# A Fourier mixing layer and a snake MLP on one Trainium2 core: the second DFT stage forward, from batch 2 on, on mirrored sums and differences in quarters of the array

## The chip, the core and the metric

The kernel runs on one core of a Trainium2 chip. The metric is device time in microseconds of one execution, and what counts is the median of several. A core has five engines with one instruction queue each: TensorE (PE in the profile; PEld is its weight load), VectorE (DVE), ScalarE (ACT), GpSimd (POOL) and SyncE (SP). An instruction waits at the head of its engine's queue until the semaphores that it names are set, and what is queued behind it waits too. In this kernel SP and POOL issue nearly all DMA transfers.

## What is computed

```python
x: (8, 3008, 256); filt_r, filt_i: (1505, 256)
X = rfft(x, axis=1)                        # along the 3008 tokens of each batch
y = irfft(X * (filt_r + 1j*filt_i), n=3008, axis=1)
h = y.reshape(24064, 256) @ w_in           # 256 -> 2048
g = h + sin(alpha*h)**2 / (alpha + 1e-9)   # snake
out = g @ w_out                            # 2048 -> 256, float32
```

## The kernel before

3008 is 47 x 64, so each transform of a batch is two matrix products with a filter between the forward and the inverse pair:

- *First stage* (`first` for batch 1 at L203, `first_tiled` from batch 2 on at L214): a DFT over 47 rows. Its 48 result rows per token group (24 frequencies s, real and imaginary) go through PSUM into `t1_h`, and by DMA into the DRAM scratch `d1`.
- *Second stage forward* (`forward`, L238): a DFT over the 64 tokens n of a group, on rows loaded back from `d1` (`load_t2`, L233). For each of the 24 s there is one full 128x128 matmul of 256 columns against the table `d_t`: real and imaginary part of 64 tokens in, real and imaginary part of 64 frequencies out. Two s are evacuated together (L246, ACT) into `xf`, and two DMAs swap its halves into `xs` (L250).
- *Filter* (`product` L253, `cross` L261, all on DVE): p = xf * f0, then xs = xs * f1 and p = p + xs, on tiles of 128x512 in fp16, 12 of each per batch.
- *Inverse* (`inverse_tiled`, L284, from batch 2 on): the second stage back. 16 matmuls of 64x64 in the four quarters of the array, three such bursts per batch, evacuated by ACT (three) and DVE (one), then by DMA to the scratch `d2`. `load_t4` (L304) reads it back and `last` (L309) does the DFT over 47; its result lies in `y`.

The MLP is the main loop. 48 chunks of 512 (or, at every sixth place, 384) tokens take 8 steps each. A step does two blocks of `hidden` (L594): two matmuls `ph` of 512 columns, ACT takes the sine into `cos_all` (L605), and DVE forms `v` (L606) from that and from `ph` in PSUM. It also does one eighth of `project` (L610) of the chunk before: in most steps 8 matmuls `po` of 256 columns. A batch is 48 steps. While the MLP of one batch pair runs, the transforms of later batches are put between the steps.

What sets the order: nothing is scheduled at run time. `put(at, fn)` (L671) gives each piece of a transform a due step; `slot` (L735) records what is due twice per step, behind the two `hidden` blocks and behind the `project`, and takes at most one TensorE piece each time. The due steps are written out in `firsts` (L674), `inverses` (L679) and the loop at L701 to L732; `clear` (L685) moves `last` and `forward` away from the bursts in quarters of the array, and `aside` (L689) moves DVE pieces that would be due up to 1.1 steps ahead of a burst to just behind it. Each engine then takes its instructions in the recorded order.

PSUM: `hps` has 4 buffers, used in turn by the `ph` blocks and by the second half of each burst (2 buffers); `fps` has 2, for the first half of a burst, for `forward` and `last`; `ops` has 2, for `po`. So two `ph` blocks recorded behind a burst reuse the buffers of the two blocks recorded just ahead of it.

For batch 2, which has the least room, the due steps are: `first_tiled` 37.5 to 43.5, `load_t2` 45, `forward` from 51 on. For batch b from 4 on, with z = 48 b: `first_tiled` z-105.5 to z-81.5, `load_t2` from z-77 on every 12 steps, `forward` from z-65 on every 4 steps, `inverse_tiled` at z-46.5, z-30.5 and z-14.5.

Of the kernel before, what the change touches and what calls it, by code (L numbers as in the profile page):

```python
# [24 lines left out]
FUSED = 1  # L25
TILED = 2


def dft_tables():
# [22 lines left out]
    f16 = np.float16  # L52
    wf, wi = wf.reshape(N1 * 2, 2, NS, 2), 2 * wi.reshape(2, NS, 2, NR)
# [13 lines left out]
    return (eh.astype(f16), wh.reshape(NK, NR).astype(f16), wt.reshape(128, 64).astype(f16), wf.transpose(0, 2, 1, 3).reshape(NR, NK).astype(f16), wi.reshape(NK, NR).astype(f16), d,  # L67
# [4 lines left out]
def kernel(  # L72
# [11 lines left out]
    eh_host, wh_host, wt_host, wf_host, wi_host, d_host, wf0_host, wi0_host, e_host = dft_tables()  # L84
    eh_dram = nc.inline_tensor(eh_host, name="eh_tbl")
    wh_dram = nc.inline_tensor(wh_host, name="wh_tbl")
# [23 lines left out]
    t2pool = pool("t2", 4)  # L110
    xfpool = pool("xf", 3)
    ppool = pool("pp", 7)
    xspool = pool("xs", 3)
# [31 lines left out]
    eh_t = e_t[:, 0:NS // 2].rearrange("p a (b m) -> p (a b) m", m=64)  # L145
# [10 lines left out]
    def load_x(b, ch):  # L156
        xt = xpool.tile([128, 8, C], FP16, name=f"x_{b}_{ch}", tag="x")
        if b >= TILED:
            for h in range(2):
                ins = nc.gpsimd.dma_start(  # L160
                    out=xt[64 * h:64 * h + N1],
                    in_=bass.AP(tensor=x.tensor, offset=x.offset + (b * S + 32 * h + ch * 8) * C,
                                ap=[[64 * C, N1], [1, 8 * C]]))
                after(ins, marks["snake"])
            return xt
# [23 lines left out]
    class Spectral:  # L189

        def __init__(self, b):
# [6 lines left out]
            self.fused = b >= FUSED  # L198
# [15 lines left out]
        def first_tiled(self, ch):  # L214
            r0 = 8 * (ch % 2)
            for q in range(2):
                own, tag = (hps, "h") if q else (fps, "f")
                ps = [own.tile([128, 512], FP32, name=f"pa_{self.b}_{ch}_{q}_{h}", tag=tag) for h in range(2)]
                for h in range(2):
                    for c in range(2):  # L220
                        n = 4 * c + 2 * q
                        nc.tensor.matmul(out=ps[h][64 * c:64 * c + 64, :], lhsT=wt_t[64 * h:64 * h + N1],  # L222
                                         rhs=self.x[ch][64 * h:64 * h + N1, n:n + 2, :], start=True, stop=True)
                for h in range(2):
                    evac(t1_h[ch // 2][:, r0 + 4 * h + 2 * q:r0 + 4 * h + 2 * q + 2, :], ps[h], h == 0)
            d1 = self.d1.rearrange("a (h n) c -> a h (n c)", h=2)
            for c in range(2):
                n0 = (8 * ch + 4 * c) * C
                nc.sync.dma_start(out=d1[:, :, n0:n0 + 4 * C],
                                  in_=t1_h[ch // 2][64 * c:64 * c + 2 * NS, r0:r0 + 8, :]  # L230
                                  .rearrange("a (h n) c -> a h (n c)", h=2))

# [5 lines left out]
        def forward(self, u):  # L238
# [6 lines left out]
            self.xf[u] = xfpool.tile([128, 2, C], FP16, name=f"xf_{b}_{u}", tag="xf")  # L245
            nc.scalar.copy(out=self.xf[u], in_=ps)  # L246
            if self.fused:
                self.xs[u] = xspool.tile([128, 2, C], FP16, name=f"xs_{b}_{u}", tag="xs")
                for p in range(2):
                    nc.sync.dma_start(out=self.xs[u][64 * p:64 * p + 64, :, :],  # L250
                                      in_=self.xf[u][64 - 64 * p:128 - 64 * p, :, :])

        def product(self, u):  # L253
            self.p[u] = []
            for k in range(1 if self.fused else 2):
                pt = ppool.tile([128, 2, C], FP16, name=f"p_{self.b}_{u}_{k}", tag="p")
                marks["prod", u] = nc.vector.tensor_tensor(out=pt, in0=self.xf[u],  # L257
                                                           in1=f_t[k][:, 2 * u:2 * u + 2, :], op=ALU.mult)
                self.p[u].append(pt)

        def cross(self, u):  # L261
            xs, p = self.xs[u], self.p[u][0]
            nc.vector.tensor_tensor(out=xs, in0=xs, in1=f_t[1][:, 2 * u:2 * u + 2, :], op=ALU.mult)  # L263
            nc.vector.tensor_tensor(out=p, in0=p, in1=xs, op=ALU.add)  # L264

        def inverse(self, w):
            b = self.b
            pr = self.p.pop(w)
# [3 lines left out]
            for i in range(2):  # L272
                for k, pt in enumerate(pr):
                    nc.tensor.matmul(out=ps[:, i, :], lhsT=e_t[:, 2 * w + i, :],
                                     rhs=pt[:, i, :], start=(k == 0), stop=(k == len(pr) - 1))
            i0 = 2 * (w % 3)
            evac(self.g[:, i0:i0 + 2, :], ps, True if b == 1 else None)
# [5 lines left out]

        def inverse_tiled(self, w):  # L284
            g = gpool.tile([128, 4, 2, C], FP16, name=f"gt_{self.b}_{w}", tag="g")
            for q in range(2):
                own, tag = (hps, "h") if q else (fps, "f")
                ps = [own.tile([128, 2, C], FP32, name=f"pc_{self.b}_{w}_{q}_{k}", tag=tag) for k in range(2)]
                for i in range(2):
                    for k in range(2):  # L290
                        for c in range(2):
                            u = 4 * w + 2 * c + q
                            nc.tensor.matmul(out=ps[k][64 * c:64 * c + 64, i, :],  # L293
                                             lhsT=eh_t[64 * k:64 * k + 64, 2 * u + i, :],
                                             rhs=self.p[u][0][64 * k:64 * k + 64, i, :], start=True, stop=True)
                for k in range(2):
                    evac(g[:, 2 * q:2 * q + 2, k, :], ps[k], (q, k) != (1, 1))
            rows = self.d2.rearrange("a n c -> (a n) c").rearrange("(z p) c -> p z c", p=64)
            for c in range(2):
                z0 = 16 * w + 8 * c  # L300
                nc.sync.dma_start(out=rows[:, z0:z0 + 8, :],
                                  in_=g[64 * c:64 * c + 64].rearrange("p j k c -> p (j k) c"))
# [6 lines left out]
        def last(self, u):  # L309
# [8 lines left out]
            evac(y[:, cb, self.b % 2, n0:n0 + 4, :], psv)  # L318

# [167 lines left out]
    def forward_0(i):  # L487
# [5 lines left out]
        own, tag = (xspool, "xs") if i % 2 else (xfpool, "xf")  # L493
        xf0[i] = own.tile([128, 4, 128], FP16, name=f"xf_0_{i}", tag=tag)
# [141 lines left out]
    def load_half_table():  # L636

        after(nc.sync.dma_start(out=eh_t, in_=eh_dram.ap()), marks["snake"])

    put_later = [(54, load_half_table)]  # L640
# [33 lines left out]
    def firsts(b):  # L674

        return {2: (37.5, 39.5, 41.5, 43.5), 3: (49.5, 54.5, 60.5, 66.5)}.get(
            b, [48 * b - 105.5 + 8 * ch for ch in range(4)])

    def inverses(b):  # L679

        return (63.5, 73.5, 81.5) if b == 2 else [48 * b - 46.5 + 16 * w for w in range(3)]

    bursts = [at for b in range(TILED, B) for at in (*firsts(b), *inverses(b))]
# [108 lines left out]
```

## Time and profile before

| | |
|---|---|
| median of 3 runs | 779.78 us (777.6 to 784.53) |
| profiled execution: time, span in the profile | 779.97 us, 778.2 us |
| mean granted TensorE clock | 0.997 |
| TensorE, VectorE, ScalarE, GpSimd busy in the span | 98%, 85%, 78%, 48% |
| TensorE matmuls | 6039 |
| DMA bytes | 101.49 MB |
| step 0 to the last step | 38.4 us to 763.5 us |

The profile lists busy time by engine, by line and by operation, waits (who waited for what, how long, how often), the chain of work that ended last, and a timeline that merges equal instructions which follow each other (start, length from the first start to the last end, how many, and the idle time before them in brackets). Matmuls are pipelined: a row's length includes the way through the array, so the time that a group of them takes of TensorE is read from its start to the start of the next group.

### The profile page before, as it was taken

To read this page: it belongs to the slowest core of one execution; us is meant where nothing else is said; L and a number is where in the kernel's file an instruction comes from. 1 tells how busy PE (TensorE), PEld (TensorE's weight loads), DVE (VectorE), ACT (ScalarE), POOL (GpSimd) and SP (SyncE) were. 2 spreads that over 40 slices of the span, in tenths; PEclk is the share of its full clock that TensorE was granted. 3 is DMA by queue.
4 is the path that set the end of the run, shared out by engine and by line. 5 is a ranking of instruction groups with operands and counts; after the bars stand their busy time and mean duration, and the time that the engine had idled before them with its cause. 6 is when DMAs were issued, how large, how long until landed. Compare 5 with 4: busy or idle time off the path is not lost.

```text
span 778.2 us, 17224 instructions
## 1 busy us (share of the span) xinstructions
PE 763.9 (98%) x6039; PEld 517.3 (66%) x6039; DVE 658.2 (85%) x1173; ACT 610.5 (78%) x1203; POOL 371.2 (48%) x649
## 2 busy tenths in 40 slices
PE   8999999999999999999999999999999999999997
PEld 4757766666666666666666666766666666766665
DVE  6986998999988888898889988899888888787773
ACT  5798888898888877888878787788778787777762
POOL 6355554634555655455464647554464655430000
PEclk9999999999999999999999999999999999999999
DMA  9955578854765428644474536764254332411112
GB/s 227 264 110 158 119 179 240 223 137 124 188 164 133 124 58 215 157 108 128 108 202 111 141 93 147 198 150 121 72 145 111 85 72 56 135 46 34 36 41 56
DMA packets 81518, 101.49 MB, mean 130 GB/s; under 512 B 18884, under 2 KB 60864, under 8 KB 81431
## 3 DMA queue, kind: packets, MB, share of 16 engines
q0 software_dynamic: 27440, 47.29, 25.9%
q1 hardware_dynamic: 53434, 52.79, 25.3%
q8 instruction: 47, 0.77, 0.4%
q10 hardware_dynamic: 557, 0.31, 0.2%
q14 instruction: 40, 0.33, 0.1%
HBM read 56.15 MB, written 46.66 MB: 132 GB/s over the span
## 4 chain that ended last, share of the span: by engine, by line
PE 91%; DVE 4%; DMA 2%; ACT 1%; issue 1%; ACTq 0%; POOLq 0%; DVEq 0%
PE po L620 40%; PE ph L601 40%; DVE v L606 3%; PE pd L316 2%; PE pb L243 2%; PE pa L222 2%; PE pc L293 1%; PE pc L513 1%; DMA w<-in_moe_alpha_dram 1%; PE warm L437 1%; DMA d<-t_h 1%; ACT cos_all L605 1%; PE pb L491 1%; DMA t<-d 1%; PE pa L459 1%
## 5 line engine op out<-in xcount | busy, mean ns | idle before, releaser
L606 DVE SCALAR_TENSOR_TENSOR v<-cos_all,ph 128x512 f16<-128x512 f32 (+1 forms) x768 | 482.7, 671 | 96.9 <-ACT cos_all L605 93.1
L605 ACT ACTIVATE cos_all<-ph 128x512 f32<-128x512 f32 (+1 forms) x768 | 413.7, 599 | 100.3 <-PE ph L601 99.8
L665 POOL DMA_DIRECT2D out_dram<-o x530 | 292.5, 558 | 241.8 <-ACT o L630 212.6
L601 PE MATMUL ph<-y,w 128*128 128x512 f16 (+1 forms) x1536 | 389.1, 375 | 1.3 <-DVE v L606 1.1
L620 PE MATMUL po<-w,v 128*128 128x256 f16 x3008 | 389.3, 273 | 0.0
L620 PEld LDWEIGHTS <-v 128*128 128x128 f16 x3008 | 290.1, 98 | 84.2 <-issue 1.1
L601 PEld LDWEIGHTS <-w 128*128 128x128 f16 x1536 | 143.2, 98 | 113.9 <-issue 19.0
L630 ACT COPY o<-po 128x512 f32<-128x512 f32 x94 | 55.9, 595 | 7.6 <-PE po L620 7.3
L246 ACT CAST xf<-pb 128x512 f16<-128x512 f32 x84 | 50.9, 606 | 2.2 <-PE pb L243 1.4
L185 ACT CAST y<-pd 128x376 f16<-128x376 f32 (+1 forms) x86 | 41.9, 490 | 12.2 <-PE pd L316 8.8
L160 POOL DMA_DIRECT2D x<-in_x_dram x48 | 25.6, 539 | 40.5 <-DVE v L606 26.7
L185 ACT CAST t_h<-pa 128x512 f16<-128x512 f32 (+1 forms) x60 | 32.8, 589 | 12.5 <-PE pa L222 11.3
L316 PEld LDWEIGHTS <-t_a 96*128 96x128 f16 x448 | 31.4, 97 | 12.7
L264 DVE TENSOR_TENSOR p<-p,xs 128x512 f16<-128x512 f16 x84 | 35.7, 425 | 2.9
L263 DVE TENSOR_TENSOR xs<-xs,filt_t 128x512 f16<-128x512 f16 x84 | 35.1, 418 | 1.6 <-DMA xs<-xf 1.5
L257 DVE TENSOR_TENSOR p<-xf,filt_t 128x512 f16<-128x512 f16 x84 | 35.0, 418 | 0.0
L185 ACT CAST gt<-pc 128x512 f16<-128x512 f32 x54 | 28.1, 594 | 8.4 <-PE pc L293 8.4
L187 DVE CAST t_h<-pa 128x512 f16<-128x512 f32 (+1 forms) x52 | 33.5, 682 | 0.2
L243 PE MATMUL pb<-t,d_t 128*128 128x256 f16 x168 | 32.1, 273 | 0.8 <-DMA t<-d 0.8
L316 PE MATMUL pd<-wh_t,t_a 96*128 96x94 f16 x384 | 31.8, 204 | 0.0
L235 POOL DMA_DIRECT2D t<-d x28 | 24.4, 873 | 13.2 <-DMA d<-t_h 11.2
L243 PEld LDWEIGHTS <-d_t 128*128 128x128 f16 x168 | 16.3, 98 | 15.3 <-DMA t<-d 1.0
(70 smaller groups left out, 277.9 us busy)
## 6 DMA issues: line engine op xcount, KB each, us to landing
t<-d POOLq DMA_DIRECT2D x28, 384.0 KB, 5.2
xs<-xf SPq DMA_DIRECT2D x168, 64.0 KB
t_a<-d SPq DMA_DIRECT2D x28, 384.0 KB
x<-in_x_dram POOLq DMA_DIRECT2D x50, 188.0 KB, 4.4
d<-t_h SPq DMA_DIRECT2D x48, 192.0 KB
d<-gt SPq DMA_DIRECT2D x36, 256.0 KB
out_dram<-o POOLq DMA_DIRECT2D x91, 64.0 KB, 2.1
out_dram<-o POOLq DMA_DIRECT2D x31, 80.0 KB, 3.8
```

The source lines that it names most:

```text
L185: marks["act"] = nc.scalar.copy(out=dst, in_=src)
L243: nc.tensor.matmul(out=ps[:, i, :], lhsT=d_t[:, s, :], rhs=self.t2[s // 6][:, s % 6, :], start=True, stop=True)
L246: nc.scalar.copy(out=self.xf[u], in_=ps)
L263: nc.vector.tensor_tensor(out=xs, in0=xs, in1=f_t[1][:, 2 * u:2 * u + 2, :], op=ALU.mult)
L264: nc.vector.tensor_tensor(out=p, in0=p, in1=xs, op=ALU.add)
L316: nc.tensor.matmul(out=psv[:, i, :], rhs=wi_t if self.b < TILED else wh_t, start=True, stop=True, lhsT=t4_h[ch // 2][0:NK, n0 % 16 + i, cb ...
L601: nc.tensor.matmul(out=ps[:, 0:n], lhsT=w1[:, cb, jb * 128:jb * 128 + 128], rhs=y_cols[:, cb, c0:c0 + n], start=(cb == 0), stop=(cb == 1))
L605: nc.scalar.activation(out=cs[:, 0:n], in_=ps[:, 0:n], func=AFT.Sin, bias=float(np.pi / 2))
L606: marks["snake"] = nc.vector.scalar_tensor_tensor(out=v[k][:, jb, 0:n], in0=cs[:, 0:n], scalar=-1.0, in1=ps[:, 0:n], op0=ALU.add, op1=ALU. ...
L620: nc.tensor.matmul(out=pso[k][:, t % 2, :], lhsT=v[k][:, jb, 128 * t:128 * t + 128], rhs=w2[:, jb, :], start=(jb == 0), stop=(jb == 15))
L630: copy(out=o[:, i0:t % 2 + 1, :], in_=pso[k][:, i0:t % 2 + 1, :])
L665: queues[i % len(queues)].dma_start(out=bass.AP(tensor=out.tensor, offset=out.offset + t0 * C, ap=[*ap, [1, C]]), in_=o_blk[p0:p0 + rows, :])
```

## The change

From batch 2 on the class `Mirrored` takes the place of the tiled methods of `Spectral`. The array of 64 tokens is folded before the second stage: token n and token 63-n are added and subtracted. Cosines then act on sums alone and sines on differences alone, so the contraction over 64 tokens x 2 parts becomes one over 32 x 2 = 64 rows, for each parity, and a matmul of `forward` needs a quarter of the array.

- `load_x` reads the second half of the tokens so that mirrored groups arrive together; in `first` the second row half of the array runs 4 matmuls of 256 columns, in mirrored order, where it ran 2 of 512 (the first row half keeps its 2 of 512 columns). ACT evacuates three of the four PSUM tiles and DVE one; before it was two and two.
- `mirror`, new, on DVE: sum and difference of `t1_h[0]` into `t1_h[1]` (128x1024 each), two per channel group, eight per batch; each is followed by two DMAs to `d1`, where there were two per group.
- `load_t2` now loads for 8 frequencies in two DMAs, three times a batch (before: four loads of one DMA). `t2pool` goes from 4 buffers to 3.
- `forward` is three bursts of 16 matmuls 64x64 of 256 columns, all four evacuations on ACT, and then two DMAs of 256 KB that swap halves into `xs_t` (before: 24 of 64 KB).
- The filter is six DVE operations of 128x1024 per burst (`product`, `cross` and `add`, two halves a), put out one by one over the 16 steps between two `forward` bursts (for batch 2 over 8).
- `xf`, `xs` and `p` become fixed tiles; one `p` lies over `d_t`. Batch 1 keeps its way on slices of these tiles; its last `load_t2` moves from step 12.5 to 24.6.
- The tables `dh` (new) and `eh` are loaded at step 39 (before: `eh` at 54), on SP.
- New due steps, and `aside` looks 0.6 step ahead rather than 1.1. Chunks, `hidden`, `project`, `store` and `last` are unchanged.

```diff
+    dh_t = e_t[:, HS:NS].rearrange("p a (k q) -> p a k q", k=2)
+    xf_t, xs_t, p_t = [cpool.tile([128, 8, C], FP16, name=name) for name in ("xf_t", "xs_t", "p_t")]
+    p_t = [p_t, d_t[:, 0:16].rearrange("p a c -> p (a c)").rearrange("p (s c) -> p s c", c=C)]
...
+    class Mirrored(Spectral):
+        def pair(self, q, name):
+            own, tag = (hps, "h") if q else (fps, "f")
+            return [own.tile([128, 2, C], FP32, name=f"{name}_{self.b}_{q}_{a}", tag=tag) for a in range(2)]
+        def first(self, ch):
...
+            for q in range(2):
+                ps = self.pair(q, f"pa_{ch}")
+                for c in range(2):
+                    n = 4 * c + 2 * q
+                    nc.tensor.matmul(out=ps[0][64 * c:64 * c + 64], lhsT=wt_t[0:N1],
+                                     rhs=x[0:N1, n:n + 2, :], start=True, stop=True)
+                for i in range(2):
+                    for c in range(2):
+                        n = 4 * c + 2 * q + i
+                        nc.tensor.matmul(out=ps[1][64 * c:64 * c + 64, i, :], lhsT=wt_t[64:64 + N1],
+                                         rhs=x[64:64 + N1, 7 - n, :], start=True, stop=True)
+                for h in range(2):
+                    evac(t1_h[0][:, r0 + 4 * h + 2 * q:r0 + 4 * h + 2 * q + 2, :], ps[h], (q, h) != (1, 1))
+        def mirror(self, ch, e):
...
+            nc.vector.tensor_tensor(out=part, in0=t1_h[0][:, r0:r0 + 4, :], in1=t1_h[0][:, r0 + 4:r0 + 8, :],
+                                    op=ALU.subtract if e else ALU.add)
+            for c in range(2):
+                n0 = (8 * ch + 4 * c) * C
+                nc.sync.dma_start(out=rows[:, ::1 - 2 * e, e, n0:n0 + 4 * C],
+                                  in_=part[64 * c:64 * c + 2 * NS].rearrange("a n c -> a (n c)"))
+        def load_t2(self, w):
...
+            for a in range(2):
+                z0 = NS * a + 8 * w
+                nc.gpsimd.dma_start(out=self.t2[w][64 * a:64 * a + 64],
+                                    in_=self.d1[z0:z0 + 8, :, :].rearrange("z n c -> n z c"))
+        def forward(self, w):
+            for q in range(2):
+                ps = self.pair(q, f"pb_{w}")
+                for i in range(2):
+                    s = 2 * q + i
+                    for a in range(2):
+                        for k in range(2):
+                            nc.tensor.matmul(out=ps[a][64 * k:64 * k + 64, i, :],
+                                             lhsT=dh_t[64 * a:64 * a + 64, 4 * w + s, k, :],
+                                             rhs=self.t2[w][64 * a:64 * a + 64, 2 * s + k, :], start=True, stop=True)
+                for a in range(2):
+                    evac(xf_t[:, 4 * a + 2 * q:4 * a + 2 * q + 2, :], ps[a], True)
+            for p in range(2):
+                nc.sync.dma_start(out=xs_t[64 * p:64 * p + 64], in_=xf_t[64 - 64 * p:128 - 64 * p])
...
     def firsts(b):
-        return {2: (37.5, 39.5, 41.5, 43.5), 3: (49.5, 54.5, 60.5, 66.5)}.get(
-            b, [48 * b - 105.5 + 8 * ch for ch in range(4)])
+        return {2: (37.5, 39.5, 41.5, 43.5), 3: (45.5, 48.5, 56, 65.5)}.get(
+            b, [48 * b + at for at in (-119, -105.5, -100.5, -87)])
+    def mirrors(b):
+        return {2: ((38.5, 39.55), (40.5, 41.55), (42.5, 43.55), (44.5, 45.55)),
+                3: ((47, 48), (49.5, 50.5), (57.5, 60.55), (67, 72.5))}.get(
+            b, [(48 * b + e, 48 * b + o) for e, o in ((-112.5, -109.5), (-104, -100.45), (-96.5, -95), (-80.5, -77.5))])
+    def forwards(b):
+        return (52, 60, 68) if b == 2 else [48 * b - 60.5 + 16 * w for w in range(3)]
+    def filters(b):
+        return (1.5, 2.5, 3.5, 4.5, 6, 7.25) if b == 2 else (1.5, 3.5, 5.5, 7, 9, 10.5)
     def inverses(b):
-        return (63.5, 73.5, 81.5) if b == 2 else [48 * b - 46.5 + 16 * w for w in range(3)]
+        return (63, 71, 79) if b == 2 else [48 * b - 46.5 + 16 * w for w in range(3)]
...
+    put(39, load_half_tables)
...
-        for g in range(4):
-            put(12.5 if b == 1 else 45 if b == 2 else max(70, z - 77 + 12 * g), s.load_t2, g)
-        for u in range(12):
-            inv = 24 + 1.21 * u if b == 1 else 57 + 2.2 * u if b == 2 else z - 59 + 4 * u
-            fwd = inv - 6
-            fwd = clear(fwd)
-            put(fwd, s.forward, u, pe=True)
-            put(aside(fwd + (0.5 if b == 1 else 1.5)), s.product, u)
-            if s.fused:
-                put(aside(fwd + (4 if b == 1 else 4.5)), s.cross, u)
...
+            for w in range(3):
+                fwd = forwards(b)[w]
+                put(46.5 if b == 2 else max(73.5, z - 75) if w == 0 else fwd - 16, s.load_t2, w)
+                put(fwd, s.forward, w, pe=True)
+                for (fn, a), at in zip(((s.product, 0), (s.product, 1), (s.cross, 0), (s.add, 0), (s.cross, 1),
+                                        (s.add, 1)), filters(b)):
+                    put(aside(fwd + at), fn, w, a)
+                put(inverses(b)[w], s.inverse, w, pe=True)
```

## The prediction, made before the change was run

> **What bounds the kernel.** I read the page first (shares, chain), then TensorE's busy time by stretch, then the timeline of single bursts, then the waits, then the POOL queue around batch 2.
>
> ```profile
> PE 763.9 (98%) x6039; PEld 517.3 (66%) x6039; DVE 658.2 (85%) x1173; ACT 610.5 (78%) x1203; POOL 371.2 (48%) x649
> ...
> PE 91%; DVE 4%; DMA 2%; ACT 1%; issue 1%; ACTq 0%; POOLq 0%; DVEq 0%
> ```
>
> ```profile
> 100.00:150.00 50.00, 50.00 (x404) 32.96 (x402) 45.05 (x85) 42.92 (x89) 29.41 (x54) 1.00 0.82 212
> 150.00:200.00 50.00, 49.81 (x412) 33.28 (x409) 46.79 (x91) 41.71 (x82) 23.50 (x44) 1.00 0.56 136
> 400.00:450.00 50.00, 50.00 (x415) 33.09 (x413) 44.12 (x80) 40.71 (x81) 29.66 (x52) 1.00 0.52 130
> ```
>
> The first shows TensorE at 98% and as 91% of the chain. The second (columns: PE, PEld, DVE, ACT, POOL, clock, DMA share, GB/s) shows it with no idle time in the stretches where the changed code runs, at the full clock 1.00. So only TensorE's own time counts, and whatever makes it wait; VectorE (88 to 94%) and ScalarE (81 to 86%) are close behind and matter as such waits.
>
> ```profile
> 229.34 1.03 PE L601 MATMUL ph<-y,w 128*128 128x512 f16 x4
> 230.21 1.04 PE L620 MATMUL po<-w,v 128*128 128x256 f16 x8
> 231.18 0.63 PE L293 MATMUL pc<-p,e_t 64*64 64x256 f16 x16
> 231.74 1.04 PE L601 MATMUL ph<-y,w 128*128 128x512 f16 x4
> ...
> 234.52 0.38 PE L243 MATMUL pb<-t,d_t 128*128 128x256 f16 x2
> 234.74 1.04 PE L620 MATMUL po<-w,v 128*128 128x256 f16 x8
> 235.61 1.03 PE L601 MATMUL ph<-y,w 128*128 128x512 f16 x4
> ```
>
> Start to start gives the price: `ph` x4 takes 230.21 - 229.34 = 0.87 us (0.217 each); `po` x8 takes 235.61 - 234.74 = 0.87 (0.109 each), but 231.18 - 230.21 = 0.97 ahead of a burst, so 0.10 goes into the turn to quarters; the burst of 16 then takes 0.56; two `pb` take 0.22.
>
> **TensorE's own work.** Removed per batch: 24 `pb` x 0.109 = 2.62 us. Added: three bursts with the same tile shape, column count and order over quarters as L293: 3 x (0.56 + 0.10) = 1.98. Saved 0.64 per batch, 3.8 over six. There is no idle time for it to vanish in, so it counts in full: -3.8.
>
> `first` keeps 512 columns per quarter and pair of PSUM tiles, but as one matmul in the upper row half and two in the lower. No row here mixes lengths. Low end 0: the `pa` burst takes 0.56 (row 125.22 to 125.78) for two rounds of 512 columns, and in L293 a quarter takes its second 256 columns straight behind its first. High end: the 256s do not run beside the 512s, each of 48 rounds costs 2 x 0.109 more, 10.5 us. I take 0: L293, with the same quarters and the same 256s, is the nearest row.
>
> **ScalarE and VectorE.** Rows for their durations:
>
> ```profile
> L257 DVE TENSOR_TENSOR p<-xf,filt_t 128x512 f16<-128x512 f16 x84 | 35.0, 418 | 0.0
> L187 DVE CAST t_h<-pa 128x512 f16<-128x512 f32 x48 | 30.8, 682 | 0.2
> L185 ACT CAST gt<-pc 128x512 f16<-128x512 f32 x54 | 28.1, 594 | 8.4 <-PE pc L293 8.4
> L501 DVE TENSOR_TENSOR p<-xf,filt_t 128x1024 f16<-128x1024 f16 x12 | 7.5, 687 | 0.3
> ```
>
> VectorE, per batch: away go 36 operations x 0.42 = 15.1 and 4 evacuations x 0.68 = 2.7, together 17.8; in come 18 filter operations and 8 mirrors of 128x1024, 26 x 0.687 = 17.9. Nothing changes in sum. ScalarE: 12 forward evacuations stay 12, `first` gives it 4 more, +2.4 us in a batch of some 92 us; it has 14 to 19% free. Both are hidden under TensorE as long as they are late by no more than a burst leaves. That margin is what the waits show:
>
> ```profile
> PE ph L601 <- DVE v L606: 1.1, 4, 0.6
> POOL t L235 <- DMA d<-t_h: 11.2, 2, 7.1
> ```
>
> In the whole span TensorE waited for `v` four times, 1.1 us, though 42 bursts stand in it, some only two steps apart. What is new: each `forward` burst from batch 3 on stands two steps behind an `inverse` burst (z-60.5+16w against z'-46.5+16w of the same or the earlier batch), and its four copies go to ScalarE alone, 4 x 0.59 = 2.4 us in one piece where there was 0.6 every four steps. Queued behind them are the sines of the next blocks, behind these their `v`, and behind these the `ph` that reuse the buffers, four blocks later. Low end: the 1.1 us go (-1.1). High end: 15 such places lose one copy's 0.3 each, +4.5. I take 0: bursts two steps apart at the first stage of batch 2 (114.8, 118.1 us) made no wait of TensorE there.
>
> **Queues and transfers, batches 3 to 7.** The swap is 2 DMAs of 256 KB a burst, not 8 of 64 KB; SP issues fewer (per batch 6 + 16 + 6 + 4 = 32 for 24 + 8 + 6 + 4 = 42). `cross` comes 5.5 steps (some 10 us) behind its burst; evacuations 3 us, issue 1.2 (two at about 0.6 as L229's rows) and 512 KB at the 239 GB/s of 135 to 150 us, 2.2, leave 3 us. `load_t2` gets 2 DMAs x 3 (POOL issue 0.88 each, +1.8 a batch on a queue 48% busy) and is due 14.5 steps ahead of its burst. It waits on POOL for the last mirror's landing, with output stores behind it; those have three buffers of four steps each. Cost 0. If that cover went, ScalarE's copy `o` would be late next. The last load of batch 1, moved behind stores on POOL to step 24.6, has 4.3 steps (8 us) to 28.9 against a landing of 5.2 (7.5 at most): 0.
>
> **Batch 2's load, the one wait that I expect.** Here the mirrors come between the first stage and the second, and the room is not larger.
>
> ```profile
> 126.20 3.13 POOL L665 DMA_DIRECT2D out_dram<-o  x6 [2.67 <-ACT o L630]
> 133.35 3.35 POOL L235 DMA_DIRECT2D t<-d  x4 [4.02 <-DMA d<-t_h]
> 136.69 1.10 POOL L160 DMA_DIRECT2D x<-in_x_dram  x2
> ```
>
> ```profile
> 121.58 6.91 SPq L229 DMA_DIRECT2D d<-t_h  x6
> 128.53 0.58 SPq L306 DMA_DIRECT2D t_a<-d  x1
> ```
>
> ```profile
> DMA to landing us min/median/max: 3.8/5.2/7.5
> ```
>
> Before: the last store to `d1` was issued by 128.49, had landed at 133.35 (4.9 later), and the loads land in 3.8 to 7.5 us (L235). After: step 45.5 is at 129.4 (step 46 began there before); a burst of 0.66, its evacuation on VectorE 0.68 and the mirror 0.69 put the last mirror at 131.5 (a few tenths for pipelines); two issues of 0.6 on SP 132.7; +4.9 gives 137.6; POOL issues the halves 0.88 apart, the second from 138.5; +5.2 gives 143.7. TensorE wants it behind the blocks of step 52: these began at 140.26 before; one more `first` burst (0.66) and no `forward` at 51 (0.22) nor the 0.15 wait at 136 give 140.55, +0.87 = 141.4. Wait 2.3. Low end 0 (landing 3.8 and a store that lands 1 us sooner). High end: DMA runs at 228 to 239 GB/s from 115 to 150 us, and 0.77 MB of tables at step 39 and 0.38 MB of batch 3's tokens stand ahead, up to 4.8 more, with landing 7.5 also 2.3 more: 9.4. I take 2.3, since SP's and DMA's slack around 118 us swallows part of that queue.
>
> **Sum.** 779.97 - 3.8 + 2.3 = 778.5, against the profiled execution, which lies 0.19 above the median. Own bounds of this case: 779.97 - 3.8 - 1.1 = 775.1 to 778.5 + 3 = 781.5.
>
> **Rivals.**
>
> 1. *Evacuation in one piece makes TensorE wait.* The mechanism above at its high end: from a lateness of ScalarE of about one copy (0.6 us) at the start of a burst it decides, since two steps leave it (stretch rows: 14 to 19% free) some 0.6 us. 778.5 + 4.5 = 783.0, slower than before. For it: three copies in a row behind `pc` today, then four. Against it: 1.1 us of waits in all. The Trainium skill, TensorEngine Tiling (Array Packing), section PSUM Bottleneck, says that tiling speeds up TensorE but not the evacuation of PSUM, and advises to use both ScalarE and VectorE for it; here the four copies are ScalarE's alone, and by that rule this rival is the outcome. The trace so far (594 ns copies, hardly a wait) leans the other way.
> 2. *VectorE overloaded in dense stretches.* For b from 4 on, between z'-9.5 and z'-3 of the MLP's batch, six 128x1024 operations, two burst evacuations and `last` copies fall in 6.5 steps: 13 x 0.671 + 6 x 0.687 + 1.4 + 0.7 = 14.9 us, where TensorE needs 6.5 x 1.74 + 1.3 + 0.7 = 13.3. Four such stretches lose up to 1.6 each, and the eight mirrors of batch 2 from 37.5 to 45.5 (7 more operations' time less 4 evacuations, 2.8) as much again: 778.5 + 6.4 + 2.8 = 787.7. It decides once VectorE's rows cost their full length; against it, back to back `v` overlap (three in 1.99 us at 229.91 in VectorE's timeline, 0.66 each, not 0.68), and `aside` keeps pieces from right ahead of a burst.
> 3. *`first` pays for mixed lengths.* Its high end is 778.5 + 10.5 = 789. A middle form: a 256 behind a 512 may not end ahead of it, so each round is one 256 longer, 48 x 0.109 = 5.2, giving 783.7. For: one queue. Against: quarters of L293 run on their own. The Trainium skill, TensorE: Matmul & The Clock Gate, Part 3, states that matmuls end strictly in program order; the middle form is what that rule makes of this loop, and no run here mixes lengths yet.
> 4. *It does nothing or the load of batch 2 costs more than is saved*: at its high end 778.5 + 7.1 = 785.6.
>
> **Chances.** Forecast 0.58; rival 1 0.13; rival 2 0.11; rival 3 0.09; rival 4 0.09. Range: from 774, the forecast's low end less a scatter of the median of about 1 (its runs lie from 2.2 below to 4.8 above), to 786, which takes in rivals 1 and 4, the middle form of 3 and part of 2. A measurement of this kernel can tell about 1% from no change, 7.8 us. Faster by more: 0.04, since the saving and all waits seen come to 4.9. Slower by more than that (over 787.6): 0.12, rivals 2 and 3 at their ends and parts of 4. Within: 0.84.
>
> **What would show it.** Right: 240 more matmuls and 240 more weight loads; `pb` bursts of 16 in 0.56 us start to start; `pa` bursts still 0.56; TensorE waits for `v` near 1 us; one wait of `pb` for `t<-d` of 1 to 4 us near 141 us. Wrong: `pa` bursts of 0.78 or 1.0 (rival 3); `ph <- DVE v` over 4 us spread over `forward` bursts (1) or gathered near the dense stretches (2); a wait over 5 us at batch 2 (4).

## The result and the profile after

808.43 us median (803.59 to 815.31, four runs) against 780.6 (777.6 to 784.53, four runs): the ratio is 1.036, with a 95% interval of 1.0264 to 1.0456. The change makes the kernel slower by 28 us where the forecast was 1.5 us faster. The profiled execution took 805.62 us, its span is 803.6.

The page, engines' busy time and chain:

```profile
PE 770.4 (96%) x6279; PEld 516.2 (64%) x6279; DVE 658.4 (82%) x1092; ACT 623.9 (78%) x1224; POOL 376.7 (47%) x661
...
PE 74%; DMA 12%; DVE 7%; ACT 4%; issue 2%; POOL 1%; SPq 0%; ACTq 0%; DVEq 0%; POOLq 0%
```

VectorE's sum is unchanged (658.4 for 658.2), as worked out, and there are 240 more matmuls, as forecast. But TensorE, 91% of the chain before, is 74% of it now: DMA rose from 2 to 12%, VectorE from 4 to 7% and ScalarE from 1 to 4%. TensorE's busy time in the stretches of before (columns as there):

```profile
100.00:150.00 50.00, 45.05 (x381) 30.12 (x380) 42.62 (x78) 40.07 (x83) 23.61 (x44) 0.97 0.76 191
150.00:200.00 50.00, 46.88 (x404) 29.92 (x403) 43.09 (x72) 41.63 (x84) 22.74 (x44) 1.00 0.61 142
400.00:450.00 50.00, 48.62 (x412) 31.51 (x409) 41.81 (x69) 40.75 (x80) 29.41 (x53) 1.00 0.70 171
```

Where it was idle for 0.2 us at most, it now stands for 5.0, 3.1 and 1.4 us. In the first of these stretches its mean granted clock is 0.97: by the trace it is 0.50 from 130.53 to 133.94 us, and so once more from 519.65 to 523.06. Matmuls at half clock for 3.41 us lose some 1.7 us each time, together 3.4 (an estimate from these two stretches). The waits now:

```profile
POOL t L315 <- DMA d<-t_h: 18.3, 2, 12.8
...
PE ph L650 <- DVE v L655: 9.9, 14, 2.9
...
PE pa L290 <- DMA x<-in_x_dram: 4.6, 5, 1.7
...
DVE t_h L304 <- DMA d<-t_h: 3.3, 2, 2.9
PE pa L295 <- DMA x<-in_x_dram: 3.3, 5, 1.1
```

Three kinds: `ph` waits for `v` (9.9 us, 1.1 before), the first-stage bursts wait for their tokens x (4.6 + 3.3, never before), and VectorE itself waits for stores. Counted from the start of the first `ph` of a step, by the trace:

| steps | before | after | what lies there |
|---|---|---|---|
| 37 to 51 | 26.5 | 34.1 | first stage of batch 2, mirrors (0.66 is one more burst of batch 3) |
| 51 to 83 | 63.9 | 68.0 | batch 2's second stage, first stage of batch 3 |
| 83 to 276 | 369.5 | 384.0 | batches 3 to 7, 13 forward bursts, one first-stage burst fewer |
| 276 to the end | 206.7 | 206.0 | two forward bursts, no first stage |
| sum from 37 | 666.6 | 692.1 | +25.5 |

The spans differ by 25.4, so all of it lies behind step 37. The last stretch shows the saving alone: -0.7, where 20 `pb` of before (2.2 us) give way to two bursts (1.3). There a burst looks as forecast:

```profile
627.29 0.63 PE L325 MATMUL pb<-t,e_t 64*64 64x256 f16 x16
627.85 1.04 PE L650 MATMUL ph<-y,w 128*128 128x512 f16 x4
```

0.56 us from start to start. With a turn of 0.09, 18 bursts take 11.8 us of TensorE where 144 matmuls took 15.7: 3.9 saved, all of it paid back several times in waits.

### The profile page after: what moved, and what is told of

Same layout as the page of the kernel before. It is cut to its first block, busy times and chain, and to the rows that moved or that the text cites. A ratio compares the mean times of both kernels' runs of the same rounds, so it can differ in the third digit from the quotient of the medians.

```text
span 803.6 us, 17497 instructions
## 1 busy us (share of the span) xinstructions
PE 770.4 (96%) x6279; PEld 516.2 (64%) x6279; DVE 658.4 (82%) x1092; ACT 623.9 (78%) x1224; POOL 376.7 (47%) x661
## 3 DMA queue, kind: packets, MB, share of 16 engines
q0 software_dynamic: 27632, 47.29, 25.5%
## 4 chain that ended last, share of the span: by engine, by line
PE 74%; DMA 12%; DVE 7%; ACT 4%; issue 2%; POOL 1%; SPq 0%; ACTq 0%; DVEq 0%; POOLq 0%
PE po L669 34%; PE ph L650 34%; DMA x<-in_x_dram 6%; DVE v L655 5%; PE pd L273 2%; DMA w_out<-in_moe_w_out_dram 2%; ACT cos_all L654 2%; DMA d_t<-d_tbl 1%; DMA d<-t_h 1%; DMA filt_t<-in_filt_r_dram 1%; ACT xf_t L190 1%; DMA w_in<-in_moe_w_in_dram 1%; DVE t_h L304 1%; PE pc L358 1%; PE pa L295 1%
## 5 line engine op out<-in xcount | busy, mean ns | idle before, releaser
L650 PE MATMUL ph<-y,w 128*128 128x512 f16 (+1 forms) x1536 | 393.8, 375 | 11.2 <-DVE v L655 9.9
L650 PEld LDWEIGHTS <-w 128*128 128x128 f16 x1536 | 144.3, 98 | 123.4 <-issue 31.6
L190 ACT CAST t_h<-pa 128x512 f16<-128x512 f32 (+1 forms) x84 | 45.1, 599 | 11.5 <-PE pa L290 6.0
L190 ACT CAST y<-pd 128x376 f16<-128x376 f32 (+1 forms) x83 | 40.7, 490 | 13.6 <-PE pd L273 10.2
L273 PEld LDWEIGHTS <-t_a 96*128 96x128 f16 x448 | 31.6, 98 | 14.8 <-DMA t_a<-d 0.9
L190 ACT CAST xf_t<-pb 128x512 f16<-128x512 f32 x72 | 37.1, 611 | 1.6 <-PE pb L325 1.6
L304 DVE TENSOR_TENSOR t_h<-t_h 128x1024 f16<-128x1024 f16 x48 | 32.7, 685 | 3.4 <-DMA d<-t_h 3.3
L315 POOL DMA_DIRECT2D t<-d x36 | 25.5, 717 | 19.9 <-DMA d<-t_h 18.3
L192 DVE CAST t_h<-pa 128x512 f16<-128x512 f32 (+1 forms) x28 | 19.2, 685 | 7.7 <-PE pa L295 7.7
L192 DVE CAST y<-pd 128x376 f16<-128x376 f32 (+2 forms) x45 | 24.4, 543 | 1.0 <-PE pd L452 1.0
L343 DVE TENSOR_TENSOR xs_t<-xs_t,filt_t 128x1024 f16<-128x1024 f16 x36 | 24.6, 684 | 0.0
L290 PE MATMUL pa<-x,wt_t 47*64 47x512 f16 x96 | 15.8, 390 | 4.6 <-DMA x<-in_x_dram 4.6
L295 PE MATMUL pa<-x,wt_t 47*64 47x256 f16 x192 | 15.6, 277 | 3.3 <-DMA x<-in_x_dram 3.3
## 6 DMA issues: line engine op xcount, KB each, us to landing
t_a<-d SPq DMA_DIRECT2D x28, 384.0 KB
```

Source lines behind the costliest of these rows:

```text
L190: marks["act"] = nc.scalar.copy(out=dst, in_=src)
L192: marks["dve"] = nc.vector.tensor_copy(out=dst, in_=src)
L273: nc.tensor.matmul(out=psv[:, i, :], rhs=wi_t if self.b < TILED else wh_t, start=True, stop=True, lhsT=t4_h[ch // 2][0:NK, n0 % 16 + i, cb ...
L304: nc.vector.tensor_tensor(out=part, in0=t1_h[0][:, r0:r0 + 4, :], in1=t1_h[0][:, r0 + 4:r0 + 8, :], op=ALU.subtract if e else ALU.add)
L315: nc.gpsimd.dma_start(out=self.t2[w][64 * a:64 * a + 64], in_=self.d1[z0:z0 + 8, :, :].rearrange("z n c -> n z c"))
L650: nc.tensor.matmul(out=ps[:, 0:n], lhsT=w1[:, cb, jb * 128:jb * 128 + 128], rhs=y_cols[:, cb, c0:c0 + n], start=(cb == 0), stop=(cb == 1))
```

## The experiments

Each row of the table under this section gives the stretches of all kernels; the stretch ahead of step 37 varies by some 6 us between runs (starts of step 37 from 108 to 115 us) and is left out of the comparison. The last column adds up, over the 15 forward bursts from step 83 on, the time from the start of a burst to the start of the first block behind it, as far as it exceeds 0.563 us; what blocks further behind wait is not in it. Each experiment but e17_best is one execution, so the scatter is read from kernels that are alike in a stretch. Steps 37 to 51 take 33.0 to 35.7 us in the ten kernels that leave the tables and mirror places of batch 2 as the change has them; part of that is whether none, one or two stretches of 3.41 us at half clock fall there. Steps 83 to 276 take 384.0 to 388.4 in three kernels that leave the load of x late (after, e1, e2) and 376.6 to 376.9 in three with the early one (e3, e8, e16). The kernels e1, e2, e5 and e9 are the changed kernel with their edit alone; e3's early load is in all the others, and what else one has is said at its place.

**The third load of x.** In the changed kernel POOL shows this ahead of the burst at 232 us:

```profile
216.46 3.66 POOL L713 DMA_DIRECT2D out_dram<-o  x7 [2.81 <-ACT o L679]
220.11 1.43 POOL L315 DMA_DIRECT2D t<-d  x2
221.52 1.08 POOL L165 DMA_DIRECT2D x<-in_x_dram  x2
```

```profile
232.63 0.40 PE L290 MATMUL pa<-x,wt_t 47*64 47x512 f16 x2 [0.69 <-DMA x<-in_x_dram]
233.26 0.30 PE L295 MATMUL pa<-x,wt_t 47*64 47x256 f16 x2 [0.23 <-DMA x<-in_x_dram]
```

The load is due at step 83.5 (about 215.4 us), the same step as a load of t2, which is recorded first; it is issued 6 us later, behind seven stores (the first waits 2.81 us for ScalarE's `o`) and that load, and lands 11.1 us after its issue (maximum 11.3 in this kernel, 7.5 before). TensorE takes up the burst at 231.9 and waits.

```diff
-                put(22 + 4 * ch if b == 2 else firsts(b)[ch] - 8, s.load_x, ch)
+                put(22 + 4 * ch if b == 2 else firsts(b)[ch] - (12 if ch == 2 else 8), s.load_x, ch)
```

> The tokens of the third group (ch 2) are loaded 12 steps ahead of their first stage and not 8; nothing else moves. Theory T (at 8 steps that load is issued on POOL behind a load of t2 due at the same step, and moves beside t4, t2 and the swap): the waits of the bursts at 158, 232, 328, 422 and 517 us for x, with the half clock behind the last 12 us, go: span 791 to 793. Rival (the DMA engines are simply full in these stretches, and whatever is moved makes another transfer late): TensorE waits as long, for another transfer, span over 800.

Measured: 791.95 us, span 790.0; no wait for x is left, and from step 37 on 681.5 for 692.1. The largest single cause is confirmed: 10.6 us, 7.1 of them between 83 and 276. Its counterpart, e9, leaves x where it is and moves the loads of t2:

```diff
-                put(46.5 if b == 2 else max(73.5, z - 75) if w == 0 else fwd - 16, s.load_t2, w)
+                put(46.5 if b == 2 else max(73.5, z - 75) if w == 0 else fwd - 12, s.load_t2, w)
```

> The changed kernel with its loads of x as they are, 8 steps ahead; only the second and third load of t2 of a batch move from 16 to 12 steps ahead of their burst, away from the load of the third x group. If it is that load alone that holds x up: the 10 us of waits for x go as with the early load, span 790 to 793. If it is the whole traffic of that stretch (t4, swap, stores, d1): half or less goes, span 797 to 803.

Span 797.6, which taken alone would speak for the whole traffic. But from step 83 on it gains as much as the early load (376.5 and 376.9 for 384.0), so there the load of t2 on the same queue is what holds x up. It does so by the transfer more than by its place in the queue: the load shown above is issued at step 86.2 in e9 and at 86.7 in the changed kernel, but the four such loads land 6.1 to 8.4 us after their issue, not 10.2 to 11.3. Between 51 and 83 nothing is gained (71.1): batch 3's third load is due at 48, behind batch 2's loads of t2 for which POOL stands 12.8 us.

**The blocks behind forward bursts.** First the kernel without mirrors, e5: from batch 4 on the sums and differences are left out, and the bursts read the first-stage tiles themselves.

```diff
+            if self.b > 3:
+                part = t1_h[0][:, r0 + 4 * e:r0 + 4 * e + 4, :]
+            else:
...
```

> From batch 4 on VectorE's mirror operations are left out, and the stores to d1 take the unfolded rows, so the sums and differences of batches 4 to 7 are not computed; all transfers stay. Theory T (the waits of ph for v behind the forward bursts come from a mirror that VectorE does one or two steps ahead of the burst): these waits, 6.9 us in all, nearly vanish for the bursts from 215 us on; span 796 to 798. Rival 1 of the prediction (four evacuations in one piece on ScalarE): they stay within 1 us of what they are.

Waits in and directly behind forward bursts from step 83 on: 0.2 us for 4.1. The span did not fall as expected but rose (807.7), since the first-stage bursts from 83 on waited 8.9 us for x and VectorE where it was 5.2, and 51 to 83 took 3.2 us more. Here is one of the bursts:

```profile
409.34 0.63 PE L328 MATMUL pb<-t,e_t 64*64 64x256 f16 x16
409.90 1.04 PE L653 MATMUL ph<-y,w 128*128 128x512 f16 x4
```

The same burst stood at 405.61 in the changed kernel, with `ph` 0.94 behind. Then the copies that rival 1 blamed:

```diff
-                    evac(xf_t[:, 4 * a + 2 * q:4 * a + 2 * q + 2, :], ps[a], True)
+                    evac(xf_t[:, 4 * a + 2 * q:4 * a + 2 * q + 2, :], ps[a], (q, a) != (1, 1))
```

> On top of the early third load (span 790.0): the last of the four evacuations of each forward burst goes to VectorE. Rival 1 of the prediction (four copies in one piece on ScalarE): the waits behind the forward bursts shrink by more than half, span 787 or less. Theory T (they come from a VectorE that is late ahead of the burst): no change or somewhat more, span 790 to 792.

4.07 us of waits for 4.03, span 789.4: those copies are not what the first blocks behind a burst wait for. They are not free either. In two places where the blocks of the next step follow without a `project` between, a block that reuses the burst's own buffers waited 0.46 and 0.18 us for a copy `xf_t` with the early load alone, and does not wait here. Then the mirrors behind the burst:

```diff
-  ((-112.5, -109.5), (-104, -100.45), (-96.5, -95), (-80.5, -77.5))
+  ((-112.5, -108.45), (-104, -100.45), (-96.5, -92.45), (-80.5, -76.45))
```

> On top of the early third load (span 790.0): for batches 4 to 7 the three mirrors that stand one or two steps ahead of a forward burst are put right behind that burst (z-108.45, z-92.45, z-76.45 for z-109.5, z-95, z-77.5); no work is taken away. Theory T (a mirror of 0.69 us on VectorE within two steps ahead of the burst makes the v late on which the two blocks behind it wait): the waits in and behind the bursts from 215 us on, 3.7 us in the first blocks and as much as 1.7 in the second, nearly vanish, span 785 to 786. Rival (VectorE has too much to do in these stretches, wherever it stands): the waits move to the next burst, span 789 to 791.

The waits behind forward bursts fell to 0.13, as theory T had it, but those of the first-stage bursts that come three to five steps later rose from 1.9 to 7.9, and steps 83 to 276 from 376.9 to 384.8 (some 3 us of that is `last` waiting for t4). The rival is right as far as it was tried: VectorE has no room there in either place. Two runs then tried to take work off it:

```diff
-   ..., ps[h], (q, h) != (1, 1))
+   ..., ps[h], True)
...
-   ..., ps[k], (q, k) != (1, 1))
+   ..., ps[k], True)
```

The first pair of lines is the first stage (e11), both are e12.

> On top of the early third load (step 37 to the end 681.5 us): all four evacuations of each first-stage burst go to ScalarE, so that VectorE has 2.7 us less per batch. Theory V (VectorE, not ScalarE, has no room left, and lateness of VectorE is what every burst pays): the waits in and behind bursts fall by 3 us or more, step 37 to the end 676 to 679. Rival S (ScalarE's copies in one piece hold the sines up): they grow by 2 us or more, 683 to 687.

> The same, and the one VectorE copy of each inverse burst goes to ScalarE too, 2.1 us per batch more. Theory V: 673 to 678 from step 37 to the end, and the waits behind forward bursts from 215 us on under 2 us. Rival S: 685 to 690, since inverse and forward bursts two steps apart then bring eight copies in a row.

Theory V failed in both; rival S had the direction, and nearly the sums from step 37 on (685.7 and 690.4). The first-stage copy on ScalarE costs 1.6 us between 83 and 276: it leaves the waits behind forward bursts at 4.0 and takes those of the first-stage bursts from 1.9 to 3.6. The inverse copy on ScalarE more than doubles the waits behind forward bursts (9.5), and now they appear in batch 7 as well, which has no mirrors beside it:

```profile
622.51 1.19 PE L650 MATMUL ph<-y,w 128*128 128x512 f16 x4 [0.19 <-DVE v L655]
```

So ScalarE counts after all, by the copies of the *inverse* burst two steps ahead. What happens is seen in the changed kernel before the burst at 280.82 us, on ScalarE, VectorE and TensorE:

```profile
277.92 0.60 ACT L190 CAST gt<-pc 128x512 f16<-128x512 f32 x1
278.39 2.31 ACT L654 ACTIVATE cos_all<-ph 128x512 f32<-128x512 f32 x4
```

```profile
279.05 1.28 DVE L655 SCALAR_TENSOR_TENSOR v<-cos_all,ph 128x512 f16<-128x512 f32 x2 [1.14 <-ACT cos_all L654]
280.26 0.54 DVE L192 CAST y<-pd 128x376 f16<-128x376 f32 x1
280.71 0.68 DVE L304 TENSOR_TENSOR t_h<-t_h 128x1024 f16<-128x1024 f16 x1
281.31 1.28 DVE L655 SCALAR_TENSOR_TENSOR v<-cos_all,ph 128x512 f16<-128x512 f32 x2
```

```profile
280.82 0.66 PE L325 MATMUL pb<-t,e_t 64*64 64x256 f16 x16
282.05 1.19 PE L650 MATMUL ph<-y,w 128*128 128x512 f16 x4 [0.57 <-DVE v L655]
```

The inverse copies delay four sines; VectorE stands 1.14 us for the first of them; then a copy of `last` and the mirror take another 1.05 us ahead of the `v` of the blocks just before the burst; and the `ph` behind the burst reuse those blocks' buffers. My reading is that either lateness alone would fit into the margin. To test it, the inverse bursts of batches 3 to 7 were moved two steps ahead:

```diff
-   [48 * b - 46.5 + 16 * w for w in range(3)]
+   [48 * b - 48.5 + 16 * w for w in range(3)]
```

> On top of the early third load: from batch 3 on the inverse bursts stand four steps ahead of the next forward burst and not two (z-48.5+16w). If the waits behind the forward bursts need both the mirror and the inverse burst just ahead: they fall from 3.7 to under 1 us for the bursts from 215 us on, step 37 to the end 677 to 679. If the mirrors alone make them: unchanged, 681 to 682.

1.7 us for 4.0: more than half is gone, but it is not under 1, so the mirrors still make some waits without an inverse burst close ahead. The sum from step 37 on stays (681.5), as 37 to 51 was 2.1 longer in this run, with two stretches at half clock there (125.82 to 132.64 us) for one; steps 83 to 276 gained 2.1. And both taken away, by the edits of e14 and e5 together:

> The early third load, the inverse bursts four steps ahead of the next forward burst, and from batch 4 on no mirror operations on VectorE (the sums and differences of batches 4 to 7 are not computed). If lateness of ScalarE (copies of the inverse burst) and of VectorE (mirror) together make the waits behind the forward bursts: these are nearly 0 from step 83 on, and steps 83 to 276, 369.5 us before the change and 374.8 with mirrors, take 367 to 371: the saving of 2.8 in this stretch, for free mirrors, is at most as large as what is left of waits. If the waits only pass on to the first-stage and inverse bursts: 373 or more.

0.0 us in the first blocks behind forward bursts, so mirrors and inverse copies together are the cause of those waits. Yet 83 to 276 take 372.2, still 2.7 over the kernel before: the first-stage bursts, three steps or more behind a forward burst, wait 2.9 us, the inverse bursts 0.7, two later blocks 0.9 for copies `xf_t`, and most such waits bring a second of 0.17 in the next block. In that stretch the kernel before has 98 `pb` (10.7 us) where the changed one has 13 forward bursts (8.5) and a first-stage burst fewer (0.66). Even with free mirrors this saving of 2.8 is eaten.

**Batch 2.** VectorE and TensorE in the changed kernel:

```profile
125.08 0.69 DVE L304 TENSOR_TENSOR t_h<-t_h 128x1024 f16<-128x1024 f16 x1
128.64 0.69 DVE L304 TENSOR_TENSOR t_h<-t_h 128x1024 f16<-128x1024 f16 x1 [2.87 <-DMA d<-t_h]
```

```profile
129.85 1.09 PE L650 MATMUL ph<-y,w 128*128 128x384 f16 x4 [2.90 <-DVE v L655]
...
131.05 1.91 PE L669 MATMUL po<-w,v 128*128 128x256 f16 x8
132.75 0.52 PE L273 MATMUL pd<-wi_t,t_a 96*128 96x94 f16 x4
```

A mirror waits until the store from its buffer, two groups earlier, has read it; every `v` queues behind it, and TensorE stands 2.90 us. Behind that, `po` x8 takes 1.70 us (131.05 to 132.75) where 0.87 is usual.

Tables (`dh` in the upper half of `d_t`, loaded at 33; `eh` at 54; half of the second `p` moves to `e_t`) and places (`d_t` pieces for three mirrors):

```diff
-    put(39, load_half_tables)
+    put(33, load_half_table, 0)
+    put(54, load_half_table, 1)
```

> The table dh goes to a part of d_t that is free from step 32 on and is loaded at step 33, eh at 54 as before the change; nothing else moves. Theory T (the 0.77 MB of tables at step 39 hold up the stores to d1 of batch 2, VectorE's mirror waits for its buffer to be stored, and the blocks behind it wait for VectorE): the waits of TensorE between steps 42 and 50, about 6 us with the half clock that follows, fall under 2 us, and the span goes from 803.6 to about 798. Rival R (the buffers of the mirrors are too few, whatever the tables do): 2 us or less is gained, and VectorE still waits for d<-t_h.

```diff
+            if self.b == 2 and 0 <= i < 3:
+                part = d_t[:, 8 * i:8 * i + 8].rearrange("p a c -> p (a c)").rearrange("p (s c) -> p s c", c=C)
```

> Batch 2's mirrors of channel group 2 and the first of group 3 write to three pieces of d_t, so that no mirror reuses a buffer whose store is still under way; the tables stay at step 39. Theory T: VectorE no longer waits for d<-t_h (3.3 us before), but the stores stay late, so the load of batch 2 lands no sooner: 3 to 5 us gained, span 799 to 801. Rival R: all of the 6 us of steps 42 to 50 goes, span about 798.

The spans (805.0, 805.6) are no measure, since the waits for x were longer in both. Steps 37 to 51 took 31.7 and 30.2 for 34.1. The places give 3.9 us there: VectorE's wait for stores falls from 3.3 to 0.2, and the first forward burst waits for t2 instead (1.2). What the tables give alone is not shown: 31.7 lies only 1.3 below the lowest of the ten kernels without either edit, no stretch at half clock fell there in this run, and VectorE still stood 2.2 us for a store. Both, with the early load (and two of the places in `e_t`):

> On top of the early third load (span 790.0): both changes for batch 2, the tables loaded at 33 and 54 and three more places for its mirrors. Theory T (tables and few places each hold VectorE): the waits of TensorE between steps 37 and 51 fall from 5.8 us to under 1.5, and one wait of 1 to 3 us of the first forward burst of batch 2 for its load shows instead; span 785 to 788. Rival (the stores to d1 are late because SP issues them one behind the other while DMA is full): 3 us or more stay between steps 37 and 51.

37 to 51 is again 30.2, so the tables add nothing to the places there, and 51 to 83 went from 65.5 to 69.4. The span, 790.7, misses the 785 to 788 expected and is no better than with the early load alone. The wait has moved to the load of batch 2, with a stretch at half clock behind it (145.91 to 149.32 us):

```profile
142.03 0.30 PE L329 MATMUL pb<-t,d_t 64*64 64x256 f16 x2 [0.44 <-DMA t<-d]
144.64 0.62 PE L329 MATMUL pb<-t,d_t 64*64 64x256 f16 x14 [2.31 <-DMA t<-d]
```

Last, batch 1's loads of t4 behind the stores, on top of e8:

```diff
-   put(z - (9.5 if b == 1 and ch < 3 else (10.5, 10.5, 10.5, 3)[ch]), s.load_t4, ch)
+   put(z - ((9.5, 6, 2, -2)[ch] if b == 1 else (10.5, 10.5, 10.5, 3)[ch]), s.load_t4, ch)
```

> The early third load and both edits for batch 2 (steps 37 to 51 took 30.2, and the first forward burst of batch 2 then waited 3.1 us for its load), and the last three loads of t4 of batch 1 (384 KB each) at steps 42, 46 and 50, not 38.5, 38.5 and 45, behind the stores to d1 on SP. If the transfers ahead on the same queue make the stores late: that wait falls to 1.5 us or less and steps 37 to 83, 99.6 us there, take 96 to 98. If it is the chain itself (burst, copy, mirror, store, load): it stays at 2.5 to 3.5.

51 to 83 took 65.8, 37 to 83 96.0, and no wait of `pb` for batch 2's load remains. So the loads of t4 ahead on the same queue (1.15 MB) held the stores up, and the chain through the mirrors had no room for it: the last stores had landed 6.8 us after the start of step 46, where it was 8.5 in e8_batch2. That the 0.77 MB of tables did the same before they were moved is not shown.

**All together, and the best version.** A first sum, e13, is e8 with both copies on ScalarE (e12) and batch 2's bursts two steps later:

> All together: the early third load, the tables at 33 and 54, three more places for batch 2's mirrors, all burst copies on ScalarE, and batch 2's second stage two steps later (54, 62, 70 and 65, 73, 81). Theory (the fold does save 3.9 us of TensorE's work, and all the rest of the loss lies in the waits that these five edits remove): step 37 to the end 664 to 670 us against 666.6 before the change, the time 775 to 782. Rival (each edit only passes the wait on): 675 or more.

690.7 from step 37 on, span 799.2: with 9.7 us behind forward bursts it carries e12's harm, which outweighs the rest. Without it, e17 is e16 with the inverse bursts of e14 and batch 2's bursts one step later:

```diff
-        return (52, 60, 68) if b == 2 else [48 * b - 60.5 + 16 * w for w in range(3)]
+        return (53, 61, 69) if b == 2 else [48 * b - 60.5 + 16 * w for w in range(3)]
...
-        return (63, 71, 79) if b == 2 else [48 * b - 46.5 + 16 * w for w in range(3)]
+        return (64, 72, 80) if b == 2 else [48 * b - 48.5 + 16 * w for w in range(3)]
```

> The same with the inverse bursts four steps ahead of the next forward burst, and batch 2's second stage one step later (53, 61, 69 and 64, 72, 80): what came out best of each. Sum of stretches so far: 30 (37 to 51) + 65 to 66 (51 to 83) + 374.8 + 206.0 = 676 to 677 from step 37 on, 10 above the 666.6 before the change: a ratio of 1.012 to 1.016. If the fold could pay here, 1.00 or less.

788.82 us (787.82 to 789.49, four runs) against 777.74 (777.03 to 778.54, seven runs): ratio 1.0142, interval 1.0125 to 1.0159. Of the 27.8 us lost, 11.1 remain: the rest came from placing, and is undone. The kernel before stays ahead.

| kernel | 37-51 | 51-83 | 83-276 | 276-end | behind forward bursts, from 83 |
|---|---|---|---|---|---|
| before | 26.5 | 63.9 | 369.5 | 206.7 | - |
| after | 34.1 | 68.0 | 384.0 | 206.0 | 4.1 |
| e1_tables | 31.7 | 71.5 | 387.1 | 206.1 | 4.1 |
| e2_slots | 30.2 | 71.4 | 388.4 | 206.2 | 4.1 |
| e3_x_early | 33.1 | 65.5 | 376.9 | 206.0 | 4.0 |
| e5_no_mirror | 34.3 | 71.2 | 387.4 | 206.0 | 0.2 |
| e6_moved | 34.6 | 65.5 | 384.8 | 206.1 | 0.1 |
| e7_split | 34.1 | 64.9 | 375.7 | 205.9 | 4.1 |
| e8_batch2 | 30.2 | 69.4 | 376.6 | 206.1 | 3.9 |
| e9_x_order | 35.7 | 71.1 | 376.5 | 206.0 | 4.0 |
| e11_first_act | 34.9 | 66.3 | 378.5 | 206.0 | 4.0 |
| e12_both_act | 33.0 | 66.8 | 383.8 | 206.9 | 9.5 |
| e13_together | 31.6 | 67.8 | 384.5 | 206.9 | 9.7 |
| e14_inverse | 35.2 | 65.5 | 374.8 | 206.0 | 1.7 |
| e15_floor | 33.7 | 65.5 | 372.2 | 206.0 | 0.0 |
| e16_t4_later | 30.2 | 65.8 | 376.7 | 206.1 | 3.9 |
| e17_best | 30.2 | 65.0 | 375.6 | 206.1 | 1.7 |

## Why the prediction was wrong, step by step

- *TensorE's own work, -3.8*: right, 3.9 by the bursts, and -0.7 in the stretch where nothing else changes.
- *`first` at 0, rival 3*: right. Undisturbed bursts take 0.563 us for 0.558, mixed lengths or not. The rule of the Trainium skill behind rival 3 (TensorE: Matmul & The Clock Gate, Part 3, matmuls end in program order) does not show as a cost here.
- *VectorE's and ScalarE's sums*: right (DVE 658.4 for 658.2; ACT +13.4, near six times 2.4).
- *Queues and transfers, batches 3 to 7, cost 0*: this step failed, and most: 10.6 us by e3_x_early. It followed the loads of t2 and the swap and never asked where the loads of x had gone, though `firsts` moves them; two loads due in the same step on one queue were in the diff.
- *ScalarE and VectorE "hidden", I take 0*: failed, 4.1 us behind forward bursts from step 83 on, and more in those around them. Two bursts two steps apart at batch 2's first stage were taken as the nearest row; there ScalarE copied two tiles of a burst and no mirror stood between. Rival 1 named the right wait and, but for 0.64 us further behind, the wrong copies: e7 clears the forward ones, e12 and e14 point to the inverse ones, and e5 to the mirror with them. That its high end of 4.5 lies near the 4.1 is chance. The Trainium skill's rule from TensorEngine Tiling (Array Packing), PSUM Bottleneck, use both engines for evacuation, holds for the inverse burst (e12) and made next to no difference for the forward one (e7). Rival 2 had VectorE's dense stretches right in kind (e6).
- *Batch 2's load, +2.3*: failed. In the changed kernel no wait of `pb` for this load appears, since VectorE was late first. What the step missed is that mirrors reuse buffers whose stores are late: steps 37 to 51 took 34.1 - 26.5 = 7.6 us more, less one burst of 0.66. In e8_batch2, where VectorE is not held, the wait did come, 2.7 us. There the stores had landed by 137.6 (POOL's wait ended there, forecast 137.6) and the second half of the load at 144.6 (forecast 143.7), but partly by luck: the last store was issued by 130.7, not 132.7, and took 6.9 us to land, not 4.9. The sum had no term for the loads of t4 ahead, without which the wait is gone (e16).
- *Sum*: every wait was costed on its own with the room of the kernel before, and no term held the half clock that follows a long wait (some 3.4 us, estimated above). That kernel had 1.1 us of waits for `v`. My reading is that its pieces of 0.42 us, evenly spread, left room, and that equal sums in pieces of 0.69 did not; no run tests the size of the pieces alone.

Open: the split of 25.5 us among the causes is not exact, since waits for x varied by run (5.2 to 8.9 us of burst waits from 83 on in kernels that left x alone), and what makes that stretch vary was not tried. Each experiment but e17_best rests on one execution.

## What to carry to other kernels

When a kernel's bound engine is full and its helpers stand at 80 to 95%, equal sums do not mean equal time: follow the pieces that stand between a burst and the buffers that it reuses, on each helper, over the burst before as well. List every load that a new set of due steps moves, and look for two on one queue in the same step. A saving of 0.5% of the bound engine's time is lost to one late transfer per batch.

## What was not expected of the hardware

- After TensorE had stood for 2.90 us, matmuls ran at half rate: the granted clock is 0.50 from 130.53 to 133.94 us, and `po` x8 took 1.70 us, not 0.87. So too from 519.65 to 523.06, after stands of 1.28 and 1.12 us close together, and in e3_x_early from 126.00 to 129.42, after 2.06 us; in e1_tables a stand of 2.2 us at the same place was not followed by it. The Trainium skill, TensorE: Matmul & The Clock Gate, Part 1, says that an idle window of about 3.4 us halves the clock; here 2.90 us and less were followed by it.
- Two VectorE operations of 128x1024 in a row take 1.29 us where one takes 0.69 (121.23 us): each overlaps the next by some 0.08.
- With a load of t2 issued just ahead on the same queue, a load of x took 10.2 to 11.3 us to land in four batches; before, 7.5 at most.
